# Part of a token MLP made one row earlier, an eviction moved to ScalarE, a new order in the iterations with values, and other arithmetic in a weight conversion (fp32 attention and mixer, one core)

## Chip, cores and metric

One core of one Trainium2 chip. The metric is the time of one execution in microseconds (us). "PE" is TensorE, "PEld" its weight loads, "DVE" VectorE, "ACT" ScalarE, "POOL" GpSimd, "SP" SyncE.

## The reference, cut to what matters

```python
# q, k, v: (8 batches, 8 heads, 576, 64) fp32;  tau = 0.02
scores = (1/8) * q @ k.transpose(0, 1, 3, 2)
scores = where(scores >= max(scores) - tau, scores, -1e9)
attn = exp(scores - max(scores));  attn = attn / (sum(attn) + 1e-9)
x = (attn @ v) -> (8, 576, 512)
# mixer: w_tok1 (576, 256), w_tok2 (256, 576), w_ch1 (512, 1536), w_ch2 (1536, 512), float64
u = x + (relu(x.transpose(0, 2, 1) @ w_tok1) @ w_tok2).transpose(0, 2, 1)      # token MLP
out = u + relu(u @ w_ch1) @ w_ch2                                               # channel MLP
```

The float64 weights are read as 64-bit words and turned into fp32 on the chip, in 31 pieces, 26 of them of 128x512. That conversion runs beside the attention and ends about 200 us into the execution.

## The kernel before, where the change and the argument touch it

A "unit" is 128 queries of two heads. Each batch is a row of 18 units. In row 0 (units 0 to 17) PE turns the exponentials in thirds of a unit; later rows use VectorE and DMA for that. An iteration u makes the scores of unit u and the turns of unit u-2. Units 5, 8, 11, 14, 17 and 20 are "visits": there PE also multiplies the values. MLP work is cut into steps that wait in the queue `todo`; from row 1 on, each unit takes a quota of them.

```python
def on_scalar(i, part):                       # per weight piece, ScalarE
    if part == 0: nc.scalar.activation(out=lo.bitcast(I32), in_=lo, func=AF.Copy, scale=2.0**-29)
    else:         nc.scalar.activation(out=h2, in_=hi.bitcast(F32), func=AF.Square)

def on_vector(i, part):                       # per weight piece, VectorE
    if part == 0:   nc.vector.tensor_scalar(out=bits, in0=hi, scalar1=3, scalar2=0x3FFFFFFF, op0=shift_left, op1=and_)
    elif part == 1: nc.vector.scalar_tensor_tensor(out=bits, in0=hi, scalar=0xC0000000, in1=bits, op0=and_, op1=or_)
    else:           nc.vector.scalar_tensor_tensor(out=dst, in0=h2, scalar=2.0**-30, in1=dst, op0=is_ge, op1=mult)
# (operation names shortened) ... GpSimd then adds the low word

def turn(u, third):
    ...                                       # three PE transposes into a buffer of ps_tr (two buffers)
    on = nc.scalar.copy if third == 1 and u % 2 else nc.vector.tensor_copy
    on(out=eTs[key][:, 3 * third : 3 * third + 3, P * place : P * place + P], in_=ps)

def token_mlp(b):                             # returns steps: 5 transposes (tx), 2 first-layer (tok1),
    ...                                       # 8 second-layer (tok2), over all four channel blocks
def push(b):
    steps, old = token_mlp(b), list(todo)
    ...                                       # mix steps with old ones, append the channel MLP's steps
    quota = (sum(c for c, _ in todo) - (KEEP if b else KEEP_FIRST)) / (UB - 1)

for u in range(len(units) + LAG + 4):
    ...
    scores(u)
    last = False
    if due and not in_blocks(due[0][1]):
        last = values_due(u)                  # the visit's multiplications
    norm(u - 1)
    if b_now: weight(2)                       # from unit 18 on: three times two steps = two pieces a unit
    else:     weight_to(2.25 * (u - 1.5))     # three steps are one piece
    while copies: copies.popleft()()          # VectorE copies the values out of PSUM
    if last: push(0)
    ...                                       # turns of unit u-2 with their evictions
    weigh(u)                                  # softmax of unit u on ScalarE
    ...
```

## Time and profile before

| | before |
|---|---|
| median of the first three runs | 1377.46 us (1377.15 to 1379.82) |
| profiled execution | 1375.1 us, granted clock 0.988 |
| PE / DVE / ACT / POOL busy | 96 / 43 / 42 / 26 % |

The averages hide two regimes, before and after the end of the conversion; the prediction shows them with their lines.

The conversion on VectorE, from the groups of instructions of the kernel before (count; busy us, mean ns; idle before, releaser):

```profile
L205 DVE SCALAR_TENSOR_TENSOR wc<-scratch,wc 128x512 uint32<-128x512 uint32 x24 | 24.2, 1009 | 0.6
L209 DVE SCALAR_TENSOR_TENSOR wc<-h,wc 128x512 f32<-128x512 f32 x24 | 20.0, 832 | 1.1
L201 DVE TENSOR_SCALAR wc<-scratch 128x512 uint32<-128x512 uint32 x24 | 14.2, 590 | 1.8 <-DMA scratch<-in_moe_w_ch_dram 1.8
```

### The profile page before, as it was taken

To read this page: it belongs to the slowest core of one execution; us is meant where nothing else is said; L and a number is where in the kernel's file an instruction comes from. 1 tells how busy PE (TensorE), PEld (TensorE's weight loads), DVE (VectorE), ACT (ScalarE), POOL (GpSimd) and SP (SyncE) were. 2 spreads that over 40 slices of the span, in tenths; PEclk is the share of its full clock that TensorE was granted. 3 is DMA by queue.
4 is the path that set the end of the run, shared out by engine and by line. 5 is a ranking of instruction groups with operands and counts; after the bars stand their busy time and mean duration, and the time that the engine had idled before them with its cause. 6 is when DMAs were issued, how large, how long until landed. Compare 5 with 4: busy or idle time off the path is not lost.

```text
span 1375.1 us, 17691 instructions
## 1 busy us (share of the span) xinstructions
PE 1322.7 (96%) x6226; PEld 817.9 (59%) x6226; DVE 588.2 (43%) x1017; ACT 581.8 (42%) x1288; POOL 356.0 (26%) x683
## 2 busy tenths in 40 slices
PE   6877799999999999999999999999999999999998
PEld 3444465646565666565665567565656576575675
DVE  6788875445444443434244444434333453201000
ACT  5666654454445444443434444353333444120110
POOL 4555653222222222222122222222121222100000
PEclk9988999999999999999999999999999999999999
DMA  5434655454544354433344435434433442400000
GB/s 121 98 96 125 183 142 124 100 123 98 122 109 114 82 121 94 113 88 95 77 100 94 113 77 123 106 83 98 103 87 75 107 103 63 115 1 16 8 11 21
DMA packets 278871, 128.20 MB, mean 93 GB/s; under 512 B 200896, under 2 KB 271552, under 8 KB 278784
## 3 DMA queue, kind: packets, MB, share of 16 engines
q1 hardware_dynamic: 150176, 111.06, 32.0%
q10 hardware_dynamic: 128608, 16.01, 7.3%
q8 instruction: 50, 0.82, 0.3%
q14 instruction: 37, 0.30, 0.1%
HBM read 43.25 MB, written 9.44 MB: 38 GB/s over the span
## 4 chain that ended last, share of the span: by engine, by line
PE 85%; DVE 7%; DMA 2%; SPq 2%; ACT 1%; issue 1%; POOL 1%; ACTq 0%; DVEq 0%; POOLq 0%
PE c L486 26%; PE c L470 26%; PE sc L302 11%; PE pv L413 9%; PE t L441 5%; PE t L448 3%; PE pv L408 3%; DVE mx L307 2%; SPq L374 2%; PE tx L432 1%; PE c L482 1%; DMA eT<-T 1%; PE tr L353 1%; DVE wc L205 1%; ACT e L317 1%
## 5 line engine op out<-in xcount | busy, mean ns | idle before, releaser
L307 DVE TENSOR_REDUCE mx<-sc 128x1 f32<-128x576 f32 x288 | 204.5, 751 | 487.9 <-PE sc L302 487.5
L470 PE MATMUL c<-xT,wc 128*128 128x256 f32 (+1 forms) x1920 | 399.4, 362 | 2.1 <-DVE xT L452 1.2
L486 PE MATMUL c<-wc,g 128*128 128x512 f32 x864 | 390.5, 597 | 0.0
L470 PEld LDWEIGHTS c<-xT,wc 128*128 128x128 f32 x1920 | 334.5, 191 | 71.5 <-issue 27.6
L308 POOL TENSOR_SCALAR bias<-mx,toff 128x1 f32<-128x1 f32 x288 | 82.8, 288 | 799.3 <-DVE mx L307 742.3
L317 ACT ACTIVATE e<-sc,bias 128x576 f32<-128x576 f32 x288 | 199.6, 739 | 162.0 <-POOL bias L308 161.4
L486 PEld LDWEIGHTS c<-wc,g 128*128 128x128 f32 x864 | 157.8, 190 | 175.7 <-issue 174.0
L471 ACT ACTIVATE g<-c 128x256 f32<-128x256 f32 (+1 forms) x240 | 86.7, 362 | 334.1 <-PE c L470 317.9
L324 ACT ACTIVATE e<-e,ntau 128x576 f32<-128x576 f32 x288 | 220.7, 771 | 0.0
L335 POOL TENSOR_SCALAR e<-e,rr 128x576 f32<-128x576 f32 x288 | 215.6, 761 | 15.8 <-DVE rr L332 4.3
L302 PE MATMUL sc<-kT,qT 64*128 64x288 f32 (+1 forms) x1280 | 196.6, 447 | 11.1 <-DVE kT L284 7.1
L365 DVE STREAM_TRANSPOSE T<-e 128x1152 f32<-128x1152 f32 x126 | 172.1, 1366 | 6.3 <-DMA eT<-T 2.6
L302 PEld LDWEIGHTS sc<-kT,qT 64*128 64x128 f32 (+1 forms) x1280 | 107.4, 184 | 98.3 <-issue 59.1
L413 PE MATMUL pv<-eT,lv 128*64 128x384 f32 (+1 forms) x1024 | 136.8, 409 | 0.0
L413 PEld LDWEIGHTS pv<-eT,lv 128*64 128x64 f32 x1024 | 76.1, 138 | 51.0 <-issue 43.6
L491 DVE COPY o<-c 128x512 f32<-128x512 f32 x36 | 24.9, 692 | 177.5 <-PE c L486 177.5
L418 ACT COPY xT<-pv 128x384 f32<-128x384 f32 (+1 forms) x56 | 21.0, 401 | 157.5 <-PE pv L413 157.5
L448 PE MATMUL t<-w,a 128*128 128x288 f32 x256 | 75.2, 421 | 7.2 <-DVE xT L452 5.3
L441 PE MATMUL t<-x_sb,w 128*128 128x512 f32 x160 | 72.1, 598 | 0.0
L448 PEld LDWEIGHTS t<-w,a 128*128 128x128 f32 x256 | 45.6, 191 | 32.2 <-issue 11.4
L452 DVE TENSOR_TENSOR xT<-xT,t 128x288 f32<-128x288 f32 x64 | 28.2, 446 | 80.5 <-PE t L448 80.0
L324 ACT ACTIVATION_READ_ACCUMULATOR e<-e,ntau 128x1 f32 x288 | 56.5, 196 | 0.0
(44 smaller groups left out, 554.7 us busy)
## 6 DMA issues: line engine op xcount, KB each, us to landing
eT<-T SPq DMA_DIRECT2D x672, 108.0 KB, 2.2
scratch<-in_moe_w_ch_dram SPq DMA_DIRECT2D x24, 512.0 KB, 3.7
lv<-in_v_dram SPq DMA_DIRECT2D x32, 288.0 KB, 3.3
out_dram<-o SPq DMA_DIRECT2D x36, 256.0 KB, 2.2
lk<-in_k_dram ACTq DMA_DIRECT2D x111, 72.0 KB, 2.6
lq<-in_q_dram ACTq DMA_DIRECT2D x106, 72.0 KB, 2.3
lq<-in_q_dram SPq DMA_DIRECT2D x22, 72.0 KB, 3.2
lk<-in_k_dram SPq DMA_DIRECT2D x17, 72.0 KB, 3.3
```

What stands on the lines that cost most here:

```text
L302: nc.tensor.matmul(sc[h][rows, f, 0:HS], lhsT=qT[r, cols], rhs=kT[r, HS * f : HS * f + HS], start=True, stop=True)
L307: nc.vector.tensor_reduce(out=mx[:, c], in_=sc[h][:, :, 0:HS], axis=AX.XY, op=ALU.max)
L317: nc.scalar.activation(out=eh, in_=sc[h][:, :, 0:HS], func=AF.Prelu, bias=bias[:, h : h + 1], scale=SCALE, alpha=STEEP)
L324: nc.scalar.activation(out=eh, in_=eh, func=AF.Exp, bias=ntau, accum_out=rs[:, h : h + 1])
L335: nc.gpsimd.tensor_scalar(out=eh, in0=eh, scalar1=rr[:, h : h + 1], scalar2=1.0, op0=ALU.mult, op1=ALU.mult)
L365: nc.vector.transpose(out=T[:, :, place, :].rearrange("p a (c x) -> p c a x", c=NK), in_=e.rearrange("p (c a x) -> p c a x", c=NK, a=4))
L413: nc.tensor.matmul(to[r], lhsT=lv[:, j, :], rhs=e[j], start=False, stop=(c == NI - 1), skip_group_check=True)
L441: nc.tensor.matmul(ps, lhsT=w1[:, t, P * m : P * m + P], rhs=x_sb[:, t, :], start=(t == 0), stop=(t == NT - 1))
L448: nc.tensor.matmul(ps, lhsT=s["a"][:, m, P * c : P * c + P], rhs=w2[:, m, HS * f : HS * f + HS], start=(m == 0), stop=(m == NTK - 1))
L470: nc.tensor.matmul(ps, lhsT=wc1[:, j, c, :], rhs=uT[:, c, GR * i : GR * i + n], start=(c == 0), stop=(c == NCC - 1))
L471: nc.scalar.activation(out=s["g"][:, j, 0:n], in_=ps, func=AF.Relu)
L486: nc.tensor.matmul(flat, lhsT=s["g"][:, j, P * t : P * t + P], rhs=wc2[:, j, :], start=False, stop=(j == NJ - 1), skip_group_check=True)
```

## The change

Its intent: relieve VectorE, which paces the early part, and bring the first token MLP, a burst at unit 20, into row 0. It has four parts:

1. *Conversion.* Abs for Square, and a form in which two of VectorE's three operations are single-tensor.
2. *Eviction.* The middle third of a turn is always evicted by ScalarE, not in odd units only.
3. *Order.* In a visit, conversion steps and the unit's softmax go ahead of the values' copies and the turns.
4. *Early token MLP.* For the first two of four channel blocks of batch 0 it is cut into nine steps; six are made in row 0 and shortly after it (units 12, 13, 15, 16, 18, 19), one at a time between units; three stay for the push at unit 20.

The diff, cut to its core:

```diff
-                nc.scalar.activation(out=h2, in_=hi.bitcast(F32), func=AF.Square)
+                nc.scalar.activation(out=h2, in_=hi.bitcast(F32), func=AF.Abs)
...
             if part == 0:
+                nc.vector.tensor_scalar(out=h2, in0=h2, scalar1=2.0**-15, scalar2=2.0**16, op0=ALU.max, op1=ALU.mult)
+            elif part == 1:
                 nc.vector.tensor_scalar(
-                    out=bits, in0=hi, scalar1=3, scalar2=0x3FFFFFFF, op0=ALU.logical_shift_left, op1=ALU.bitwise_and
+                    out=bits, in0=h2.bitcast(U32), scalar1=3, scalar2=0, op0=ALU.logical_shift_left, op1=ALU.bitwise_or
                 )
             else:
-                nc.vector.scalar_tensor_tensor(out=dst, in0=h2, scalar=2.0**-30, in1=dst, op0=ALU.is_ge, op1=ALU.mult)
+                nc.vector.scalar_tensor_tensor(
+                    out=bits, in0=hi, scalar=0x80000000, in1=bits, op0=ALU.bitwise_and, op1=ALU.bitwise_or
+                )
...
-        on = nc.scalar.copy if third == 1 and u % 2 else nc.vector.tensor_copy
+        on = nc.scalar.copy if third == 1 else nc.vector.tensor_copy
...
-    def token_mlp(b):
+    def token_mlp(b, ps=range(NP)):
...          (every step works on the channel blocks in ps; a first layer is 128*len(ps) columns wide;
...           before unit 18 its PSUM is a buffer of ps_tr)
+    early = deque()
     def push(b):
-        steps, old = token_mlp(b), list(todo)
+        steps, waits = token_mlp(b) if b else token_mlp(b, range(NP // 2, NP))
+        old = list(todo)
         todo.clear()
+        todo.extend(early)
+        early.clear()
...
             values(b, p0, g)
+            if b == 0 and p0 == 0 and g == 2:
+                return True
...
+        visit = False
         if due and not in_blocks(due[0][1]):
+            visit = due[0][0] <= u
             last = values_due(u)
+        elif early:
+            early.popleft()[1]()
...
-            weight_to(2.25 * (u - 1.5))
+            weight_to(2.25 * (u - (1 if visit else 1.5)))
+            if visit and on:
+                weigh(u)
         while copies:
             copies.popleft()()
-        if last:
+        if last and u < UB:
+            early.extend(token_mlp(0, range(NP // 2))[0])
+        elif last:
             push(0)
...
-        if on:
+        if on and (b_now or not visit):
             weigh(u)
```

More of the change, by code (lines that the diff above doesn't have):

```diff
@@ L200, in on_vector @@
             if part == 0:
+                nc.vector.tensor_scalar(out=h2, in0=h2, scalar1=2.0**-15, scalar2=2.0**16, op0=ALU.max, op1=ALU.mult)
+            elif part == 1:
                 nc.vector.tensor_scalar(
-                    out=bits, in0=hi, scalar1=3, scalar2=0x3FFFFFFF, op0=ALU.logical_shift_left, op1=ALU.bitwise_and
-                )
-            elif part == 1:
-                nc.vector.scalar_tensor_tensor(
-                    out=bits, in0=hi, scalar=0xC0000000, in1=bits, op0=ALU.bitwise_and, op1=ALU.bitwise_or
-                )
-            else:
-                nc.vector.scalar_tensor_tensor(out=dst, in0=h2, scalar=2.0**-30, in1=dst, op0=ALU.is_ge, op1=ALU.mult)
+                    out=bits, in0=h2.bitcast(U32), scalar1=3, scalar2=0, op0=ALU.logical_shift_left, op1=ALU.bitwise_or
+                )
+            else:
+                nc.vector.scalar_tensor_tensor(
+                    out=bits, in0=hi, scalar=0x80000000, in1=bits, op0=ALU.bitwise_and, op1=ALU.bitwise_or
+                )
     def on_gpsimd(i):
@@ L420, in values, with psum, turn_x @@
                 copies.append(lambda x=x, ps=ps: nc.vector.tensor_copy(out=x, in_=ps))
-    def token_mlp(b):
-        xT = xTs.pop(b)
+    hidden = {}
+    def token_mlp(b, ps=range(NP)):
+        xT = xTs[b]
         o = S * (b % 2)
-        s = {}
-        def turn_x(t):
-            M = MT[t]
-            ps = ps_tr.tile([P, MAIN], F32, tag="tr", name=f"tx_{b}_{t}").rearrange("p (c x) -> p c x", c=NP)
-            for p in range(NP):
-                nc.tensor.transpose(out=ps[0:M, p, :], in_=xT[:, p, o + t * P : o + t * P + M], identity=ident)
-            nc.scalar.copy(out=x_sb[0:M, t, :], in_=ps[0:M].rearrange("q p d -> q (p d)"))
+        L = len(ps)
+        cols = slice(P * ps[0], P * ps[0] + P * L)
+        if b not in hidden:
+            hidden[b] = work.tile([P, NTK, DM], F32, tag="a", bufs=1, name=f"a_{b}")
+        a = hidden[b]
+        def psum(name):
+            return (ps_mm or ps_tr).tile([P, DM], F32, tag="mm" if ps_mm else "tr", name=name)
+        def turn_x(t, n):
+            M = MT[t]
+            to = ps_tr.tile([P, MAIN], F32, tag="tr", name=f"tx_{b}_{t}_{ps[0]}")[0:M, 0 : n * L * P].rearrange("p (t c x) -> p t c x", t=n, c=L)
+            for i in range(n):
+                for c in range(L):
+                    tok = o + (t + i) * P
+                    nc.tensor.transpose(out=to[:, i, c, :], in_=xT[:, ps[c], tok : tok + M], identity=ident)
+            nc.scalar.copy(out=x_sb[0:M, t : t + n, cols], in_=to.rearrange("q t p d -> q t (p d)"))
@@ L435, in tok1 @@
         def tok1(m):
             need(2)
-            if m == 0:
-                s["a"] = work.tile([P, NTK, DM], F32, tag="a", bufs=1, name=f"a_{b}")
-            ps = ps_mm.tile([P, DM], F32, tag="mm", name=f"t1_{b}_{m}")
+            to = psum(f"t1_{b}_{m}_{ps[0]}")[:, 0 : P * L]
             for t in range(NT):
-                nc.tensor.matmul(ps, lhsT=w1[:, t, P * m : P * m + P], rhs=x_sb[:, t, :], start=(t == 0), stop=(t == NT - 1))
-            nc.scalar.activation(out=s["a"][:, m, :], in_=ps, func=AF.Relu)
+                nc.tensor.matmul(to, lhsT=w1[:, t, P * m : P * m + P], rhs=x_sb[:, t, cols], start=(t == 0), stop=(t == NT - 1))
@@ L444, in tok2 @@
+            nc.scalar.activation(out=a[:, m, cols], in_=to, func=AF.Relu)
         def tok2(c, f):
             need(6)
-            ps = ps_mm.tile([P, HS], F32, tag="mm", name=f"t2_{b}_{c}_{f}")
+            to = psum(f"t2_{b}_{c}_{f}")[:, 0:HS]
             for m in range(NTK):
                 nc.tensor.matmul(
-                    ps, lhsT=s["a"][:, m, P * c : P * c + P], rhs=w2[:, m, HS * f : HS * f + HS], start=(m == 0), stop=(m == NTK - 1)
+                    to, lhsT=a[:, m, P * c : P * c + P], rhs=w2[:, m, HS * f : HS * f + HS], start=(m == 0), stop=(m == NTK - 1)
@@ L450, in tok2 @@
                 )
             u = xT[:, c, o + HS * f : o + HS * f + HS]
-            nc.vector.tensor_add(out=u, in0=u, in1=ps)
-        steps = [(0.44, lambda t=t: turn_x(t)) for t in range(NT)]
-        steps += [(4.3, lambda m=m: tok1(m)) for m in range(NTK)]
-        steps += [(0.97, lambda c=c, f=f: tok2(c, f)) for c in range(NCC) for f in range(2)]
-        return steps
+            nc.vector.tensor_add(out=u, in0=u, in1=to)
+        n = NI // L
+        steps = [(0.11 * n * L, lambda t=t: turn_x(t, n)) for t in range(0, NI, n)] + [(0.11 * L, lambda: turn_x(NI, 1))]
@@ L459, in channel_mlp @@
+        first = len(steps)
+        steps += [(1.1 * L, lambda m=m: tok1(m)) for m in range(NTK)]
+        steps += [(0.97, lambda c=c, f=f: tok2(c, f)) for c in ps for f in range(2)]
+        return steps, (first, first + NTK)
     def channel_mlp(b, uT, i):
@@ L519, in push @@
         uT = xTs[b]
-        steps, old = token_mlp(b), list(todo)
+        steps, waits = token_mlp(b) if b else token_mlp(b, range(NP // 2, NP))
+        old = list(todo)
         todo.clear()
+        todo.extend(early)
+        early.clear()
         for i, step in enumerate(steps):
-            n = 2 if i in (NT, NT + NTK) else 1
+            n = 2 if i in waits else 1
             todo.extend(old[:n] + [step])
```

## The prediction

> **What bounds the kernel now.** I read the page first (its slices), then busy time by stretch, then the waits of the first 206 us, then the order of instructions in single iterations. The slices show two regimes; each digit is the busy tenths of 34.4 us:
>
> ```profile
> PE   6877799999999999999999999999999999999998
> DVE  6788875445444443434244444434333453201000
> ACT  5666654454445444443434444353333444120110
> PEclk9988999999999999999999999999999999999999
> ```
>
> From the seventh slice on TensorE is the bound. In the first six no engine is full, but VectorE is the nearest to it. I cut the span at the first scores (7.06 us), at the 19th unit's scores, where row 0 (18 units) ends (104.2 us), and where the last weight piece is converted (about 206 us). The columns after the length are busy us of PE, PEld, DVE, ACT, POOL, then the granted clock:
>
> ```profile
> 7.06:104.20 97.14, 78.93 (x445) 47.80 (x445) 75.09 (x158) 63.66 (x134) 53.15 (x89) 0.91 0.43 100
> 104.20:206.30 102.10, 84.44 (x388) 51.95 (x388) 85.93 (x132) 64.97 (x134) 59.45 (x69) 0.92 0.58 152
> 206.30:1375.00 1168.70, 1159.31 (x5396) 718.11 (x5394) 425.06 (x721) 451.90 (x1020) 241.35 (x514) 1.00 0.37 87
> ```
>
> The third stretch has 9 us of idle PE in 1169 us: there only less PE work helps. The first two hold 18.2 + 17.7 = 36 us of idle PE, and their PE ran at a clock of about 0.91, so all that can be won lies before 206 us. What PE waits for there:
>
> ```profile
> ACT eT L355 <- PE tr L353: 23.2, 7, 6.1
> PE tr L353 <- DVE eT L355: 17.7, 8, 3.6
> DVE xT L420 <- PE pv L413: 7.7, 4, 2.9
> PE t L448 <- DVE xT L452: 4.4, 3, 2.2
> ```
>
> Two patterns follow. In an iteration with values ("visit": units 5, 8, 11, 14, 17, 20) ScalarE sits idle behind the eviction of a transpose that PE reaches only after the values, although its softmax work for the unit is ready. VectorE waits too:
>
> ```profile
> 31.06 0.43 ACT L193 ACTIVATE h<-scratch 64x256 f32<-64x256 f32 x1
> 37.60 0.48 ACT L355 COPY eT<-tr 128x384 f32<-128x384 f32 x1 [6.11 <-PE tr L353]
> ...
> 36.40 0.56 DVE L420 COPY xT<-pv 128x384 f32<-128x384 f32 x1 [2.85 <-PE pv L413]
> ```
>
> After 104 us the conversion runs at two pieces of 128x512 per unit, and PE waits for the additions of the token MLP that stand in VectorE's queue behind it (133 to 173 us: five units of 7.6 to 11.0 us). And the push of the first token MLP at unit 20 is a burst on PE between values and the next scores:
>
> ```profile
> 125.40 0.65 PE L432 MATMUL tx<-ident,xT 128*128 128x128 f32 x4
> 126.56 1.10 PE L432 MATMUL tx<-ident,xT 128*128 128x128 f32 x8 [0.51 <-DVE xT L420]
> 127.90 1.11 PE L432 MATMUL tx<-ident,xT 128*128 128x128 f32 x8 [0.24 <-ACT x_sb L433]
> 128.85 4.46 PE L441 MATMUL t<-x_sb,w 128*128 128x512 f32 x10
> 133.24 0.52 PE L302 MATMUL sc<-kT,qT 64*128 64x288 f32 x2
> ```
>
> **What the Trainium skill says.** "VectorE: DVE Perf Modes", section "The perf-mode tier table": a tensor_scalar in fp32 from SBUF reaches two elements per cycle, a two-tensor operation one. The trace agrees: by their lines, the median of the one-tensor L201 is 412 ns and of the two-tensor L205 702 ns at 512 elements. "SBUF — State Buffer", section "SBUF: two separate sides": VectorE in a 2-port mode or with two SBUF inputs and GpSimd exclude each other for a whole instruction. It agrees: the same L201 takes up to 1516 ns and L205 up to 1676 ns when GpSimd's addition (median 1412 ns) runs. "TensorE: Matmul & The Clock Gate", Part 1: an idle window halves PE's clock. It agrees: 0.69 was granted from 104.2 to 126 us, the stretch with the most idle PE.
>
> **The change part by part.**
>
> *Arithmetic of the conversion.* Before, a piece costs VectorE a tensor_scalar and two scalar_tensor_tensor: 0.41 + 0.70 + 0.69 = 1.80 us. After, two tensor_scalar and one scalar_tensor_tensor: 0.41 + 0.41 + 0.70 = 1.52 us, so -0.28 us for each of 26 pieces of 512 columns, about -0.15 for the five small ones: 8 us of VectorE in all. The time lost to GpSimd (means of 590, 1009 and 832 ns over the medians, 0.63 us a piece) stays, as all three operations can still be blocked. On ScalarE Abs replaces Square (667 ns; the order of the built kernel shows still one table load). New is that the first VectorE step of a piece needs that Abs; by the order, the Abs mostly precedes the unit's softmax or is one iteration old, so I count no cost.
>
> *Eviction of the middle third.* ScalarE takes it in all 18 units, not in 9: VectorE -9 x 0.55 = -5 us, ScalarE +9 x 0.48 = +4.3 us. It also frees a transpose buffer without waiting for VectorE's maxima: units after an eviction by ScalarE took 3.1 to 4.8 us (units 7, 9, 13, 15), those after VectorE's 4.6 to 6.1 (6, 10, 12, 18).
>
> *Order in visits.* Both activations of the unit (two of 1.4 and 1.5 us a pair) go ahead of the eviction, into the 5 to 6 us in which ScalarE idled; the conversion steps also go ahead of the values' copies. PE itself is full in a visit (unit 5: scores, values, transposes from 30.1 to 38.0 us without a gap), so the visit stays as long; the unit after it starts with ScalarE and VectorE free, worth some 0.6 us each (in unit 6 the maxima started at 39.7 where scores could have allowed 39.1).
>
> *Token MLP of the first two channel blocks.* By the order it is popped in units 12, 13, 15 (transposes), 16, 18 (first layer), 19 (one step of the second); three steps stay for the push at unit 20. PE work moved ahead of unit 20: 10 of 20 transposes of a 2.9 us total (1.4), two half first layers (10 entries of 0.227 us, from the 24 of a 256-column group in 5.45 us: 2.3 each, 4.5), one second-layer step (half of 2.21 us: 1.1): 7 us. Halving the first layer costs 4 x 2.27 - 2 x 4.46 = 0.2 us, nothing. The price lies in row 0: a first-layer step holds a transpose buffer and, through its in-order Relu, ScalarE for 2.3 us in units 16 and 18, and a transposing step 0.65 us of PE and 0.58 us of ScalarE in three units.
>
> **The sum**, from the bottom:
> - To 104 us: eviction and order -6 us (six visits at 0.6, some 2.5 from units no longer waiting for VectorE), inserted steps +3: **-3**.
> - 104 to 133 us (units 18 to 20): conversion and evictions -1; the burst at unit 20 of 7.8 us becomes 10 transposes, a half layer and three second-layer steps, 1.8 + 2.3 + 3.3 = 7.4, with fewer waits: **-2** together.
> - 133 to 173 us: VectorE is full; eight pieces by 0.28 us is 2.2, three of the eight additions gone from the queue 1.3, the 1.9 us in which ScalarE waited for a first layer of 512 columns halved, PE's waits for additions of 4.4 us mostly gone: **-6**.
> - 173 to 206 us: **-1**.
> - The channel MLP of row 0 now starts about an iteration sooner, so row 1's quota falls by (18.6 - 12.3)/17 = 0.37 us a unit over its ten PE-bound units: **-4**.
>
> Together -16 us. From the top: VectorE loses 13 of its 161 busy us before 206 us; at its present share of 0.81 that is 13/0.81 = 16 us. I take 1377.5 - 15.5 = **1362 us**.
>
> **Rivals.**
> 1. *ScalarE becomes the bound of row 0.* A plain unit there asks of it 2.9 us of softmax, 0.9 of conversion, 0.48 of eviction: 4.3 us, and the inserted steps add 2.5 in all. For: units of 3.1 us cannot then repeat. Against: 63.7 busy of 97 us leaves room, and visits take some. Then row 0 gets longer by 2 to 4 us and the whole is 1367 to 1371.
> 2. *VectorE waits for Abs.* From unit 18 on a piece's Abs and its first VectorE step are issued back to back, behind evictions that wait for PE. For: ScalarE already waited 13.6 us for weight loads. Against: VectorE gets there late. One us in each of nine units: 1371.
> 3. *More than counted.* PE, busier in row 0, keeps its clock: the slow stretch from 109 to 123 us is worth up to 5 us, and units without VectorE's buffer wait could all become 4 us: 1350 to 1354.
> 4. *Hidden anyway*: row 0's PE sum (78.9 + 7 of 97 us at this clock) becomes its bound and the moved work only changes place: 1368.
>
> **Range and chances.** Rivals 1, 2 and 4 set the upper end, 3 the lower: 1350 to 1372 us. Two per cent is 1349.9 us, 27.5 us less; that takes three quarters of the 36 us of idle PE, so faster by over 2% has 0.09. Slower by over 2% would need PE work in the bound stretch, which the change doesn't add: 0.01. The rest, 0.90.
>
> **What will show it.** Right: the shift at about 0.41 us, the 70.8 us of conversion on VectorE (the sums of its three lines) falling by some 8; scores of unit 18 near 101 us, of unit 25 near 162 (172.9 before); the eviction's 23 us of waiting on ScalarE mostly gone; PE busy after the conversion unchanged. Wrong: VectorE waiting for Abs, ScalarE over 80% busy in row 0, units 16 and 18 longer than 7 us, or an idle PE of over 30 us still before the last conversion.

## The result, and the profile after

| | before | after |
|---|---|---|
| median, same rounds, five runs each | 1379.32 us (1377.15 to 1382.49) | 1361.22 us (1359.68 to 1363.54) |
| ratio after/before | | 0.9866 (95% interval 0.9844 to 0.9888) |
| profiled execution | 1375.1 us | 1357.6 us |
| PE busy / VectorE busy / ScalarE busy, us | 1322.7 / 588.2 / 581.8 | 1314.2 / 576.6 / 585.5 |

A ratio here and below is the mean time of a kernel's fast runs over that of the other's fast runs of the same rounds, so not quite the ratio of the medians. The change saved 1.3%, some 18 us. All outputs are right. The prediction was 1362 us, a saving of 15.5 us counted from the 1377.5 us of the first three runs.

The slices of the changed kernel (33.9 us each) fill up one slice earlier:

```profile
PE   6888999999999999999999999999999999999998
DVE  6889864454444434443333454434333443201000
ACT  6776655445454444543434445343434444120010
PEclk8998999999999999999999999999999999999999
```

The same three stretches of the changed kernel, cut at the first scores, at the 19th unit's scores (to half a us) and at the end of the conversion. The columns after the length are busy us of PE, PEld, DVE, ACT, POOL, then granted clock, DMA share, GB/s:

```profile
7.06:97.90 90.84, 74.96 (x460) 47.74 (x461) 71.54 (x153) 72.24 (x153) 53.01 (x89) 0.94 0.46 108
97.90:189.00 91.10, 82.51 (x394) 53.65 (x394) 78.00 (x129) 59.02 (x123) 56.88 (x69) 0.94 0.62 162
189.00:1357.00 1168.00, 1156.72 (x5396) 715.21 (x5392) 424.95 (x721) 452.99 (x1024) 242.15 (x514) 1.00 0.37 88
```

Before the conversion ends PE now idles 15.9 + 8.6 = 24.5 us, not 36. The PE-bound rest is as long as it was (1168 us). The waits of the changed kernel in its first 190 us (us in total, times, longest us):

```profile
ACT eT L356 <- PE tr L354: 9.1, 9, 2.0
PE tr L354 <- ACT eT L356: 7.6, 10, 1.4
...
DVE h L202 <- ACT h L194: 6.8, 2, 3.6
...
PE tr L354 <- DVE eT L356: 1.9, 2, 1.6
```

ScalarE's wait ahead of the eviction fell from 23.2 to 9.1 us, PE's wait for VectorE's eviction from 17.7 to 1.9 us; in return its waits for ScalarE's evictions grew from 3.1 to 7.6 us. New is the third line: VectorE waits for the Abs. It does so in two units only; here is the wait in unit 24 (from the timeline: start, length, engine, instruction, what it waited for):

```profile
154.79 0.70 ACT L192 ACTIVATE scratch<-scratch 128x512 int32<-128x512 uint32 x1 [5.21 <-DMA scratch<-in_moe_w_ch_dram]
156.09 0.43 DVE L202 TENSOR_SCALAR h<-h 128x512 f32<-128x512 f32 x1 [3.22 <-ACT h L194]
```

ScalarE waited for a weight piece that had not landed, and VectorE behind it. In the visit of unit 5 the softmax (L318 and, left out here, L325) now precedes the eviction, as intended:

```profile
32.13 1.34 ACT L318 ACTIVATE e<-sc,bias 128x576 f32<-128x576 f32 x2
...
35.83 0.48 ACT L356 COPY eT<-tr 128x384 f32<-128x384 f32 x1 [0.84 <-PE tr L354]
```

And what is left of the burst at unit 20 on PE: three second-layer steps (L459), 10 transposes (L445, 1.5 us, left out here), half a first layer (L452), then the scores:

```profile
118.57 3.18 PE L459 MATMUL t<-w,a 128*128 128x288 f32 x12
...
123.10 2.32 PE L452 MATMUL t<-x_sb,w 128*128 128x256 f32 x10
125.36 1.24 PE L303 MATMUL sc<-kT,qT 64*128 64x288 f32 x8
```

The conversion of the changed kernel on VectorE, by groups: two operations without a second tensor (L202, L204), one with it (L208).

```profile
L204 DVE TENSOR_SCALAR wc<-h 128x512 uint32<-128x512 uint32 x24 | 19.0, 790 | 0.6
L208 DVE SCALAR_TENSOR_TENSOR wc<-scratch,wc 128x512 uint32<-128x512 uint32 x24 | 18.2, 759 | 0.4
L202 DVE TENSOR_SCALAR h<-h 128x512 f32<-128x512 f32 (+2 forms) x31 | 17.9, 577 | 6.8 <-ACT h L194 6.8
```

**A stage table for all runs.** To place a gain I took the start of each unit's first row maximum on VectorE (L307 before, L308 after) from the trace and formed the length of groups of units. The first maximum itself starts anywhere from 9.4 to 11.7 us, with the landing of the first loads, whatever the kernel; so stages are counted from it. For unit 25, for instance, it is at 174.13 us before and at 161.25 after. The columns are units, the entries us.

| kernel (one profile each) | 0-11 | 12-16 | 17-20 | 21-24 | 25-26 | 27-29 | 30 to end |
|---|---|---|---|---|---|---|---|
| before | 62.1 | 28.3 | 34.7 | 39.6 | 17.3 | 21.9 | 1161.7 |
| after | 56.9 | 27.1 | 33.4 | 34.4 | 16.1 | 19.6 | 1160.7 |
| e9 (after again) | 57.0 | 27.2 | 33.2 | 34.8 | 16.1 | 19.8 | 1160.6 |
| e1 no early MLP | 58.4 | 27.1 | 35.9 | 38.7 | 16.1 | 23.4 | 1160.3 |
| e2 old eviction | 60.9 | 27.8 | 34.0 | 35.3 | 17.0 | 18.5 | 1160.4 |
| e3 old order | 59.5 | 30.5 | 33.5 | 34.3 | 17.6 | 18.6 | 1160.4 |
| e4 old conversion | 58.9 | 27.6 | 36.2 | 35.8 | 17.3 | 18.9 | 1160.3 |
| e5 early MLP alone | 62.1 | 28.0 | 34.8 | 35.0 | 17.3 | 19.1 | 1161.0 |
| e6 conversion alone | 64.6 | 29.3 | 34.1 | 38.3 | 16.1 | 23.3 | 1161.4 |
| e7 eviction and order | 57.9 | 29.1 | 34.9 | 38.9 | 17.3 | 21.8 | 1161.3 |
| e8 e1 with idle PE work | 57.1 | 27.4 | 34.6 | 38.6 | 16.1 | 22.8 | 1162.1 |
| e10 after, PE work at unit 20 | 58.0 | 27.4 | 34.5 | 37.3 | 16.1 | 23.9 | 1160.7 |
| e11 all early | 58.2 | 28.2 | 35.6 | 42.5 | 16.1 | 19.5 | 1173.6 |
| e12 all early, faster conversion | 59.0 | 29.5 | 36.0 | 45.3 | 14.7 | 19.1 | 1172.1 |

Stretches at half the clock, multiples of some 3.4 us long (one to four of them together), fall at other places in each execution; one that lies wholly in a visit makes that unit about 2 us longer (unit 14 took 8.6 us in e6 and e7, which have 3.4 us of it there, and 6.6 in e5, which has none). So differences of 2 us in the first three columns are not to be read; the last four columns repeat within 0.5 us (after and e9). In the profile before, such stretches cover parts of units 5 and 11, which took 8.0 us each; they took 6.9 and 6.6 in the changed kernel, whose profile has none there (its own slow stretch lies in unit 2, 8.9 us against 8.1).

### The profile page after: what moved, and what is told of

Same layout as the page of the kernel before. It is cut to its first block, busy times and chain, and to the rows that moved or that the text cites. A ratio compares the mean times of both kernels' runs of the same rounds, so it can differ in the third digit from the quotient of the medians.

```text
span 1357.6 us, 17717 instructions
## 1 busy us (share of the span) xinstructions
PE 1314.2 (97%) x6246; PEld 816.6 (60%) x6246; DVE 576.6 (42%) x1008; ACT 585.5 (43%) x1300; POOL 354.1 (26%) x683
## 4 chain that ended last, share of the span: by engine, by line
PE 86%; DVE 6%; DMA 2%; ACT 2%; SPq 2%; issue 1%; POOL 1%; ACTq 0%; DVEq 0%; POOLq 0%
PE c L499 27%; PE c L483 26%; PE sc L303 10%; PE pv L414 8%; PE t L452 5%; PE t L459 4%; PE pv L409 3%; SPq L375 2%; DVE mx L308 2%; PE tx L445 1%; PE c L495 1%; DMA lk<-in_k_dram 1%; ACT e L318 1%; ACT e L325 1%; PE tr L354 1%
## 5 line engine op out<-in xcount | busy, mean ns | idle before, releaser
L308 DVE TENSOR_REDUCE mx<-sc 128x1 f32<-128x576 f32 x288 | 204.3, 750 | 482.8 <-PE sc L303 482.8
L318 ACT ACTIVATE e<-sc,bias 128x576 f32<-128x576 f32 x288 | 199.5, 740 | 157.5 <-POOL bias L309 154.8
L325 ACT ACTIVATE e<-e,ntau 128x576 f32<-128x576 f32 x288 | 221.0, 771 | 0.0
L336 POOL TENSOR_SCALAR e<-e,rr 128x576 f32<-128x576 f32 x288 | 215.1, 760 | 14.7 <-DVE rr L333 3.0
L303 PE MATMUL sc<-kT,qT 64*128 64x288 f32 (+1 forms) x1280 | 190.5, 432 | 12.4 <-DVE kT L285 7.1
L303 PEld LDWEIGHTS sc<-kT,qT 64*128 64x128 f32 (+1 forms) x1280 | 105.3, 177 | 98.7 <-issue 60.6
L459 PE MATMUL t<-w,a 128*128 128x288 f32 x256 | 75.7, 423 | 5.7 <-DVE xT L463 4.8
L452 PE MATMUL t<-x_sb,w 128*128 128x512 f32 (+1 forms) x180 | 72.4, 549 | 0.0
L459 PEld LDWEIGHTS t<-w,a 128*128 128x128 f32 x256 | 46.4, 194 | 28.4 <-issue 11.7
L325 ACT ACTIVATION_READ_ACCUMULATOR e<-e,ntau 128x1 f32 x288 | 56.7, 197 | 0.0
```

What stands on the lines that cost most here:

```text
L303: nc.tensor.matmul(sc[h][rows, f, 0:HS], lhsT=qT[r, cols], rhs=kT[r, HS * f : HS * f + HS], start=True, stop=True)
L308: nc.vector.tensor_reduce(out=mx[:, c], in_=sc[h][:, :, 0:HS], axis=AX.XY, op=ALU.max)
L318: nc.scalar.activation(out=eh, in_=sc[h][:, :, 0:HS], func=AF.Prelu, bias=bias[:, h : h + 1], scale=SCALE, alpha=STEEP)
L325: nc.scalar.activation(out=eh, in_=eh, func=AF.Exp, bias=ntau, accum_out=rs[:, h : h + 1])
L336: nc.gpsimd.tensor_scalar(out=eh, in0=eh, scalar1=rr[:, h : h + 1], scalar2=1.0, op0=ALU.mult, op1=ALU.mult)
L452: nc.tensor.matmul(to, lhsT=w1[:, t, P * m : P * m + P], rhs=x_sb[:, t, cols], start=(t == 0), stop=(t == NT - 1))
```

## The experiments

The theory that the runs were to test was the ledger of the prediction: VectorE's relief and the order make most of the gain, the early MLP gives some and costs some. Its rival: the early MLP makes the most.

### One part undone at a time

**e1: without the early token MLP.**

```diff
-            if b == 0 and p0 == 0 and g == 2:
-                return True
...
-        steps, waits = token_mlp(b) if b else token_mlp(b, range(NP // 2, NP))
+        steps, waits = token_mlp(b)
```

> The changed kernel with the whole token MLP of row 0 again at the push of unit 20; the other three parts stay. My theory (the parts add up as in the prediction): the inserted steps cost row 0 some 3 us and give back 4 us of quota in row 1 and 1 to 2 us at unit 20, so without them unit 18's maxima come 2 to 3 us earlier than in the changed kernel (99.8 us), unit 20 is over 12 us long again, and the whole is 2 to 4 us slower than the changed kernel: ratio to the kernel before 0.988 to 0.990. Rival (the moved work is the whole gain): ratio 0.995 or above. Rival (it only changes place): ratio 0.985 to 0.987.

Measured: 1373.52 us (1370.96 to 1375.11), ratio to before 0.9956 (0.9940 to 0.9971). So undoing this one part gives back 0.9866 → 0.9956, about 12 us of the 18. My own expectation fails and the rival's holds. The table says where: units 12 to 16, in which four of the six extra steps stand, take 27.1 us with them and without; the prediction had put a cost of 3 us there. Units 18 and 19, with the other two, take 16.1 us together with them and 15.8 without. The gain is 4.3 us in units 21 to 24 and 3.8 us in 27 to 29; the rest lies in the first columns, where single profiles don't place it.

**e2: with the old eviction.**

```diff
-        on = nc.scalar.copy if third == 1 else nc.vector.tensor_copy
+        on = nc.scalar.copy if third == 1 and u % 2 else nc.vector.tensor_copy
```

> The changed kernel with the middle third of even units evicted by VectorE again. Theory: the transpose of the last third then waits for VectorE's maxima again in units 4, 6, 10, 12, 16; these are 4.5 to 5.5 us long again instead of 3.5 to 3.9, unit 18's maxima come 3 to 5 us later than 99.8 us, ratio 0.989 to 0.991. Rival (evictions lie beside other work, only VectorE's sum of 5 us counts little): units 6, 10, 12 stay below 4.2 us and the ratio is 0.986 to 0.988.

Measured: 1367.79 us, ratio 0.9912 (0.9895 to 0.9928), as expected: 6 us lost. Units 4, 6, 10 and 12 are back at 5.5, 4.2, 5.6 and 4.8 us, from 3.8, 3.5, 3.5 and 3.9 in the changed kernel.

**e3: with the old order in visits.**

```diff
-            weight_to(2.25 * (u - (1 if visit else 1.5)))
-            if visit and on:
-                weigh(u)
+            weight_to(2.25 * (u - 1.5))
...
-        if on and (b_now or not visit):
+        if on:
             weigh(u)
```

> The changed kernel with the softmax of a visit again behind the evictions, and the old pace of conversion there. Theory: units after a visit (6, 9, 12, 15) start with ScalarE and VectorE late by 0.6 us and the visits get 1 us longer; unit 18's maxima come 3 to 5 us later than 99.8 us, ratio 0.988 to 0.991. Rival (PE fills the visit, the order is worth nothing): unit 18 within 1 us of 99.8 and ratio 0.986 to 0.987.

Measured: 1365.52 us (1360.45 to 1368.93), ratio 0.9897 (0.9875 to 0.9919). That is about 4 us lost, as expected, but the interval overlaps that of the changed kernel (0.9844 to 0.9888), so the loss isn't clear of noise. Units after a visit (6, 9, 12, 15) took 4.5, 4.8, 4.1 and 5.4 us, where the changed kernel has 3.5, 4.5, 3.9 and 4.0.

**e4: with the old conversion.**

```diff
-                nc.scalar.activation(out=h2, in_=hi.bitcast(F32), func=AF.Abs)
+                nc.scalar.activation(out=h2, in_=hi.bitcast(F32), func=AF.Square)
...          (and the three old VectorE operations put back)
```

> The changed kernel with the old arithmetic of the conversion. Theory: VectorE is busy some 8 us longer before the last conversion, little of it in row 0 (below 2 us at unit 18) and most in units 21 to 26, the last conversion ends 4 to 6 us later than 186.8 us, ratio 0.989 to 0.991. Rival (the new first step's dependence on ScalarE costs what the arithmetic saves: VectorE waited 6.8 us for it in the changed kernel): ratio 0.984 to 0.987.

Measured: 1367.29 us, ratio 0.9909 (0.9890 to 0.9929). The size is as expected, not the place: by the table, 2.7 us of it lies in units 21 to 26, and the rest in stages where the profiles differ by chance as much. What the part is worth in row 0 stays open.

The four single losses, 12, 6, 4 and 6 us, add up to 29 us, more than the 18 that the whole brings. So they are not shares of the gain; why they overlap isn't shown.

### One part alone

Each is the changed kernel with several of the edits above made together: **e5, early token MLP alone** (the edits of e2, e3 and e4); **e6, conversion alone** (e1, e2 and e3); **e7, eviction and order** (e1 and e4).

> The kernel before with the early token MLP alone. Undoing it cost 0.0090 of the ratio (0.9956 against 0.9866), and the four undone parts together cost more than the whole change brings, so the parts help each other. Theory (each engine of row 0 has to be relieved for any to count): alone it brings less than it cost to lose, 3 to 7 us, ratio 0.995 to 0.998. Rival (the parts are independent and the four single losses are noise): 11 us or more, ratio 0.992 or below.

> The kernel before with the new arithmetic of the conversion alone (undone it cost 0.0043). Theory: VectorE still waits in visits and behind evictions, so it brings 1 to 4 us, ratio 0.997 to 0.999, with the last conversion 3 to 5 us earlier than 200.0. Rival (VectorE's sum divided by its share: 8/0.81): 8 to 10 us, ratio 0.993 to 0.994.

> The kernel before with evictions and order of the changed kernel, old arithmetic and token MLP. Theory: these two make row 0 shorter by 3 to 5 us (even units near 3.9, visits 1 us shorter), but what is won there comes back only where VectorE and PE are the bound later: 3 to 5 us in all, ratio 0.996 to 0.998, unit 18 at 101 to 103 us after correction of the start. Rival: both are worth their undone losses of 0.0046 and 0.0031, ratio 0.992.

Measured against before: e5 1370.03 us, 0.9924 (0.9908 to 0.9940); e6 1379.30 us, 0.9988 (0.9967 to 1.0009); e7 1375.11 us, 0.9960 (0.9944 to 0.9976). With before at about 1380 us that is 10.5, 1.7 and 5.5 us; the sum, 17.7, is nearly the 18.5 of the whole. The times of e6 and e7 came as I had expected; for e5 the rival was nearly right and I was wrong. For e6 I had also expected the last conversion 3 to 5 us earlier than at 200.0 us; in its profile, whose row 0 has more of the slow clock, it ended at 203.3.

e6 is the instructive one. It takes 10 us of conversion off VectorE (the sums of the three lines, 70.8 us before and 60.8 in e6), and the whole gains 1.7, by the interval at most 4.6 and perhaps nothing. In its profile the two VectorE-bound stages are 1.3 + 1.2 = 2.5 us shorter (0.6 us for a unit with two pieces, as twice 0.28 says: unit 25 went from 8.85 to 8.25), and units 27 to 29 are 1.3 us longer: PE has the same work to do (67.9 us busy in units 21 to 29, 68.0 before), and takes it there. One part of this stays open: in e6 VectorE also waits for the new Abs, the longest time in unit 27 (4.1 us), and no run separates what these waits cost. The line, for the first 210 us (us in total, times, longest us):

```profile
DVE h L202 <- ACT h L194: 8.7, 6, 4.1
```

Nor does e6 agree with e4, in which taking the same arithmetic out of the whole lost 6 us; why isn't shown.

### Is it the clock, or PE's work?

By e1 and e5 the early MLP is the largest part. Two mechanisms could do it: the extra PE work in row 0 keeps the granted clock up (rival 3 of the prediction), or PE work has left a stretch in which it costs time.

**e8: e1, with unread PE work where the early steps stood.** Transposes and multiplications of the same size, results never read.

```diff
-        elif early:
-            early.popleft()[1]()
+        elif u in WARM:              # {12: 0, 13: 0, 15: 1, 16: 2, 18: 2, 19: 3}
+            idle_pe(u)               # 4, 4, 2 transposes, 5 matmuls of 256 columns twice, 2 of 288
```

> The kernel without the early token MLP (0.9956), with as many matmuls of the same shapes at the same places in units 12 to 19 whose results nobody reads. If the early work helps by keeping PE's clock up: the slow clock of 13.7 us at units 18 to 20 is gone, units 20 and 21 fall to some 11 and 8 us, and the ratio comes down to 0.990 to 0.992. If it helps because the work itself is gone from units 20 to 24 and from row 1: ratio 0.995 to 0.998, unit 20 stays at 12 us or more, units 22 and 23 at 9.5.

Measured: 1373.62 us, ratio 0.9947 (0.9929 to 0.9964), where e1 had 0.9956: the intervals cover each other. One of the inserted groups, in the profile of e8:

```profile
86.72 2.43 PE L563 MATMUL idle<-xT,ident 128*128 128x256 f32 x10
```

Mean granted clock of the two executions, first e1, then e8:

```profile
core 0: 1371.4 us, clock 0.990
```

```profile
core 0: 1368.7 us, clock 0.996
```

In the six runs of each the mean clock was 0.990 and 0.995, and the time was the same. In the profile of e8 unit 20 took 11.0 us (12.6 in e1), as the clock's mechanism foretold, but the ratio didn't follow. Some 8 us of extra PE work (the sum of the inserted groups) and the higher clock together came to nothing. In units 12 to 16, where none of the three profiles has a slow stretch, the extra work cost at most 0.3 us (27.4 us, against 27.1 in e1). In units 18 to 20 the two effects can't be told apart by e8; e10 below settles the main part.

**e9: the changed kernel again,** as a yardstick.

> The changed kernel once more, on the chip and in the rounds of the next three: ratio 0.985 to 0.988. It is the yardstick; a value outside says that the ratios of different calls may not be compared to a few tenths of a per cent.

Measured: 1362.89 us (1358.37 to 1366.97), ratio 0.9869 (0.9847 to 0.9891); the first time it was 0.9866.

**e10: the changed kernel, with 7 us of unread PE work put back at the push of unit 20.**

```diff
+        if b == 0:
+            steps, waits = idle_steps(uT) + steps, (5, 11, 13)
```

(10 transposes, two half first layers, one second-layer step, with the costs that the quota counts for such steps.)

> The changed kernel with the early token MLP where it is, but 7 us of PE work of the same shapes put back at the push of unit 20, unread and without evictions or additions. If what the early step saves is PE work in units 20 to 24 and in row 1: the 10 us are lost again, ratio 0.994 to 0.997, units 21 to 26 together 54 to 55 us instead of 50.4. If it saves because evictions and additions left the queues of ScalarE and VectorE there: ratio 0.987 to 0.990 and units 21 to 26 together 50 to 52 us.

Measured: 1370.31 us, ratio 0.9925 (0.9903 to 0.9947); 7.7 us of the early MLP's 12 are gone. In the profile the work stands ahead of unit 21's scores (L303) and behind them:

```profile
124.42 0.49 PE L538 MATMUL idle_t<-ident,xT 128*128 128x128 f32 x3
125.13 0.98 PE L538 MATMUL idle_t<-ident,xT 128*128 128x128 f32 x7 [0.22 <-DVE xT L463]
125.95 2.32 PE L543 MATMUL idle<-xT,ident 128*128 128x256 f32 x10
...
129.37 3.40 PE L543 MATMUL idle<-xT,ident 128*128 128x256 f32 x14
```

The table shows the same two stages hit that e1 hits: units 21 to 24 take 37.3 us (34.4 without; e1 38.7), units 27 to 29 23.9 (19.6; e1 23.4). The mean clock of its runs was 0.993, that of the changed kernel 0.993 and 0.995 (e9), so the clock doesn't explain the loss. So most of the early MLP's gain is 7 us of PE work, with the quota counted for it, taken out of the stretch from unit 20 on and put where PE idled. That stretch was not full: in units 21 to 29 PE was busy for 68.0 us and idle for 10.9 before, 64.7 and 5.3 in the changed kernel, 67.8 and 9.5 in e10. Idle time of PE, between steps that wait for one another, comes and goes with the work and is over half of the gain there; why was not tested. What is left of the 12, about 4 us, isn't separated: the additions that VectorE no longer has to make there, the halved first layers, or the spread of the runs.

### Does more of it help?

If row 0 takes six steps for nothing, why not all nine, or a faster conversion as well?

**e11: all nine early steps before unit 20** (two each in units 12, 18 and 19). **e12: the same, and 2.5 conversion steps per unit of row 0** in place of 2.25, at both places.

```diff
-        elif early:
-            early.popleft()[1]()
+        else:
+            for _ in range(min(len(early), {12: 2, 18: 2, 19: 2}.get(u, 1))):
+                early.popleft()[1]()
```

> All nine steps of the first two channel blocks within row 0 (two in units 12, 18 and 19), where the changed kernel leaves three second-layer steps to unit 20. Three steps are 3.3 us of PE work. If seven us moved bring 10 and row 0 has room: 2 to 4 us more, ratio 0.983 to 0.985. If row 0 is full: units 12, 18 and 19 get longer by what is added and the ratio stays at 0.986 to 0.988.

> The same with 2.5 conversion steps a unit in row 0 instead of 2.25: 42 of 93 steps done at unit 18 instead of 38. VectorE gets 2.7 us more in row 0 and 2.7 less after. If VectorE's queue is as much the bound in row 0 as after it: within 1 us of the kernel without it. If row 0 has room: 1 to 3 us faster, and the waits for weight loads in units 24 and 27 (3.2 and 3.6 us in the changed kernel) get shorter.

Measured: e11 1382.64 us, ratio 1.0016 (0.9994 to 1.0038); e12 1388.68 us, 1.0069 (1.0043 to 1.0095). Every expectation fails: 20 us and more are lost to the changed kernel. In the table most of the loss of e11 stands in two places (its profile is the slowest of its six runs, and the first three columns add 4.6 us, within their chance). Units 21 to 24 are 8.1 us longer, nearly all of it in unit 24 (17.9 us; 10.1 in the changed kernel). And units 30 to the end take 13 us more. For unit 24 the timeline of e11 shows the chain:

```profile
148.97 11.99 SPq L375 DMA_DIRECT2D eT<-T  x16
161.08 1.98 SPq L177 DMA_DIRECT2D scratch<-in_moe_w_ch_dram  x4
164.62 0.65 ACT L192 ACTIVATE scratch<-scratch 128x512 int32<-128x512 uint32 x1 [6.94 <-DMA scratch<-in_moe_w_ch_dram]
165.85 0.43 DVE L202 TENSOR_SCALAR h<-h 128x512 f32<-128x512 f32 x1 [6.33 <-ACT h L194]
...
167.50 1.05 PE L483 MATMUL c<-xT,wc 128*128 128x256 f32 x2 [4.98 <-ACT g L484]
```

SyncE issues the 16 transfers that rearrange a turned block for 12 us (some 0.6 us each, and about 2 us of waits between them); only then can it issue the loads of the next weight pieces. ScalarE, which converts them, waits 6.9 us for the first, VectorE 6.3 us for ScalarE, and PE, out of other steps, 5 us. The changed kernel has the same 16 transfers (10.6 us from 140.13) and the same wait, 5.2 us on ScalarE and 3.2 on VectorE; but PE there still has steps to fill it. In e12 the wait fell into unit 23, which took 14.9 us (7.9 in the changed kernel). That PE was one stage further ahead in the MLP and so asked for the weights earlier is how I read it; no run separates it. The second loss, after unit 30, I only located: 9 of the 13 us are idle PE (17 us from the conversion's end to PE's last instruction, 8 in the changed kernel); of the 17, 5.7 are waits for loads of k and 4.3 for rearranged blocks. Why a different cut of row 1 moves those waits stays open.

No kernel tried is faster than the changed one.

## Why the prediction was right, step by step

The time, 1361 against 1362, was right; the ledger behind it not in every term, and the split among the parts was wrong, so that errors of both signs cancelled: in that the close hit was luck. Stages from the table, after minus before:

| term of the sum | predicted | measured | what the runs say |
|---|---|---|---|
| to unit 18 (eviction, order -6; steps +3) | -3 | -6.4 (units 0 to 17) | the +3 didn't come (e1, e8); 2.5 of the 6.4 stand in units 5 and 11, where the profile before has slow stretches and the one after has none |
| units 18 to 20 | -2 | -1.3 | small, within the chance of one profile |
| units 21 to 24 | -6 | -5.3 | early MLP -4.3 (e1), conversion -1.5 (e4), in part together |
| to the conversion's end | -1 | -1.2 (25, 26) | the conversion: two units by 0.6 us |
| row 1's smaller quota | -4 | -2.3 (27 to 29) and -1.0 after | comes at once at the end of the conversion, not spread over ten units; e10, which puts PE work and quota back, loses it again |
| sum | -16 | -17.5 | |

The scores of unit 18 began at 98.5 us (104.2 before; 101 foreseen), those of unit 25 at 158.3 (172.9; 162).

- **The mis-sized term is the cost of the early steps in row 0.** The prediction wrote "inserted steps +3"; it measured 0.0 us (27.1 and 27.1 in units 12 to 16, after and e1), and e8's unread work of the same size cost no more than 0.3. The transposes and first-layer entries fell into time in which PE would have idled; that ScalarE's share of them found room as well rests on units 12 to 16 alone. With this term the early MLP was put at 2 to 4 us in all (the expectation of e1); it brought 12 when undone and 10.5 alone.
- **The other arithmetic of the conversion.** Its 8 us of VectorE are about right: the three lines sum to 63.7 us (17.9 + 19.0 + 3.8 + 18.2 + 4.8, small forms counted), 7.1 less than 70.8; 10.0 less in e6. As a gain they are worth less alone: 1.7 us, and 0.6 us in each unit that VectorE paces. Undone from the whole they cost 6 us (e4), which the sum of the units doesn't explain.
- **So the check "from the top" was right by accident.** It divided 13 us of VectorE work by its share and called the 16 us the gain. VectorE did get 11.6 us less, but the largest part of the gain is PE work moved (e10), and the rule fails where it was tested alone: e6 took 10 us off VectorE, for which it gives 10/0.81 = 12 us, and gained 1.7, at most 4.6.
- **Eviction and order: -6 predicted, 5.5 measured** (e7), about 4 to 6 us for each when undone from the whole. The mean clock of e7's runs was also higher than before (0.9915 and 0.9875); how much of the 5.5 us is the clock was not tested.
- **Rival 1 (ScalarE becomes row 0's bound)** did not come, narrowly: it is busy 72.2 of 90.8 us, 79.5%. Of the signs named for it, unit 16 stayed under 7 us (6.9) and unit 18 is over it (8.0), but was 8.6 before.
- **Rival 2 (VectorE waits for Abs)** came in two of the units foreseen, 6.8 us in all, but as a second link: the first is a weight piece that lands late, and e4, which has no such dependence, still has ScalarE waiting for pieces (17.7 us, 17.4 in the changed kernel) and was not faster. What the waits cost in e6 (8.7 us) is open.
- **Rival 3 (the clock)** is refuted as the main cause of the early MLP's gain by e8 and e10 together; for the other parts it stands untested. **Rival 4 (hidden anyway)** is refuted by e5.
- **Two readings of the prediction don't hold.** It counts five units between 133 and 173 us; there are four (21 to 24), which its eight pieces also say. And it takes the clock of 0.69 from 104.2 to 126 us as that of the stretch with the most idle PE: from 126 to 150 us PE idled as long (6.2 of 24.0 us; 6.0 of 21.8) at a clock of 1.00.

## What to carry to other kernels

Before counting what an inserted step costs, look at whether the engine it uses is idle in that very stage: here six steps went in at no cost that could be measured, and they earned more than their PE time in the stage that they left. Work taken off a busy engine can earn much less than its size; measure it alone (1.7 us for 10) before adding it to a sum. And a slack that takes six steps need not take nine: the three more cost 20 us, some 8 of it where a late weight load met an engine with nothing left to do, most of the rest later and for a cause that stays open.

## What the Trainium skill lacked or had wrong

- "DMA: Bandwidth & Descriptors", section "Issuing engines are not separate DMA queues", calls the time that the sequencer takes to initiate a DMA "usually small relative to the DMA itself". Here 16 of them in a row took SyncE 10.6 (after) and 12.0 us (e11), some 0.6 us each beside a median of 2.3 us from issue to landing, and a weight load behind them kept ScalarE waiting for 5.2 us (after) and 6.9 us (e11).
- "SBUF — State Buffer", section "SBUF: two separate sides", states the lock between VectorE and GpSimd, and slowdowns of single instructions, but no mean cost in a mixed stream. Here L204, the single-tensor operation that took 0.43 us unhindered, took 1.40 us where GpSimd's addition had started first (at 105.77 us, for instance), and 0.79 us in the mean of 24.
- "TensorE: Matmul & The Clock Gate", Part 1, says that the window runs freely and that the penalty differs from run to run. The traces agree: the slow stretches lie elsewhere in each profile. It has no figure for a slow stretch inside a kernel of mixed work: here one of 3.4 us within a visit cost about 2 us (unit 14: 8.6 us in e6 and e7, 6.6 in e5).
- No page gives the spread of a kernel's start: in these 14 profiles the first maximum began from 9.4 to 11.7 us, and in two profiles of one kernel (after and e9) at 9.5 and 10.3. That is as much as some parts of this change are worth.
